# Output stores on two queues, and one store instead of two for the last tokens of both halves

## The chip, the cores and the metric

The kernel runs on one core of one Trainium2 chip. The metric is device time in microseconds (us), lower is better. Executions of one kernel mostly agree within a few tenths of a per cent. Each run is marked fast or slow by its time; of all runs told here one was slow, and only fast ones are compared.

## The reference, cut to what matters

The input `x` has 8 batches of 4224 tokens of 192 float32 values. A causal convolution of 7 taps with softmax weights per head is followed by a token-by-token mixing matrix, a relu and an output projection. The result has the shape of `x`, so 26 MB come in and 26 MB go out.

```python
x_unf = x_pad[:, idx, :].reshape(B, S, K, H, group)      # 7 shifted copies
x = einsum('hk,bskhg->bshg', w, x_unf).reshape(B, S, D)  # per-head convolution
W_tok = scale * einsum('bsd,btd->bst', x @ w_q, x @ w_k)
out = maximum(einsum('bst,btd->bsd', W_tok, x), 0.0) @ w_out
```

## The kernel before

The kernel treats each batch as two halves of 2112 tokens. Its output leaves in pieces numbered `n = 5 * b + i`: four tiles of 512 tokens of both halves (`i` 0 to 3, one store of 768 KB each) and a remainder (`i == 4`), the last 64 tokens of each half, as two stores of 48 KB. In the last batch tile 3 is the last to be computed and leaves as four quarters, in order to start storing before all of it is there. This is the code that makes the stores, all on SyncE's queue (`"sp"`):

```python
at = (b * S + 512 * i) * D
if rem:
    parts = [(at + h * HALF * D, [[D, 64], [1, D]], OUT[64 * h : 64 * h + 64, orr, 0, 0:D])
             for h in range(2)]
elif tail:
    parts = [(at + q * D, [[4 * D, 128], [HALF * D, 2], [1, D]], ...)]      # a quarter
else:
    parts = [(at, [[4 * D, 128], [HALF * D, 2], [1, 4 * D]], OUT[:, orr, :, :])]
for at, dims, src in parts:
    st = P.dma("sp", lambda e, ...: e.dma_start(bass.AP(out_t, at, dims), src), og[orr], evs + wait)
```

`dims` is the access pattern in DRAM, outermost dimension first, as `[step, count]`. `OUT` has 128 partitions and `NO = 8` slots: the copy that fills a slot waits until the store of eight pieces earlier has landed. Two more couplings matter below. Some stores also wait for loads (`GATES`, cut below): piece 10 is held back until the first loads of batch 6 have landed. And SyncE issues in order, so a store held back holds back all that follow.

```python
GATES = {0: 8, 3: 9, 5: 10, 10: 12, 15: 14}   # store n waits for a group of loads
...
P.op("sp", lambda e: e.nop(), og)             # the kernel's end: every store has landed
```

## Time and profile before

| what | before |
|---|---|
| time, median of 3 runs | 153.7 us (153.67 to 154.07) |
| profiled span | 152.5 us (of an execution of 154.32 us) |
| TensorE busy | 92% of the span |
| last copy into an output slot ends | 146.4 us |
| from there to the end | 6.1 us |

The prediction shows the slices, the chain and the windows. Two more views answer to lines shown later. First the page's DMA parts: the row of SyncE's hardware queue (packets, MB, share of 16 engines) and two groups of stores (count, KB each, median us from issue to landing).

```profile
q1 hardware_dynamic: 12576, 27.14, 48.9%
...
out_dram<-o_sb SPq DMA_DIRECT2D x31, 768.0 KB, 7.2
...
out_dram<-o_sb SPq DMA_DIRECT2D x16, 48.0 KB, 6.3
```

The packet count is worth remembering: data packets plus one 4-byte packet for each engine that reports a DMA done. Second, the rows of all output stores (duration of the issue in ns, minimum/median/maximum), and what SyncE waited for between 60 and 100 us (total, times, longest).

```profile
L860 SPq DMA_DIRECT2D out_dram<-o_sb x51: 372/514/2103, 49.0 to 149.1; - x51
```

```profile
SPq L166 <- DMA xw<-in_x_dram: 25.5, 2, 14.0
```

The longest wait of the last line, 14.0 us, is the gate of piece 10. SyncE got past it and issued that store at 84.10 us.

### The profile page before, as it was taken

Reading aid. Unit: us, or ns where it says so; the run is one execution under the profiler, and the core shown is the slowest. Engines: PE = TensorE matmul, PEld = TensorE weight load, DVE = VectorE, ACT = ScalarE, POOL = GpSimd, SP = SyncE. Lnnn points to the kernel's source line nnn. Section 1 sums busy time; section 2 is a strip of 40 time slices with the busy share of each in tenths; the row PEclk is TensorE's granted clock in tenths of the full one; section 3 lists DMA queues with packets and bytes.
Section 4 is the critical chain, followed back from the end, with each engine's and each line's share of the span. In section 5 each row is a group of like instructions: output and inputs, shape, how many; then the busy total and the mean of one; then the engine's idle time right before and its main releaser. Section 6 shows DMA issues by size and latency. Waiting matters only on the chain.

```text
span 152.5 us, 5699 instructions
## 1 busy us (share of the span) xinstructions
PE 140.1 (92%) x2457; PEld 101.3 (66%) x2457; DVE 120.3 (79%) x240; ACT 127.7 (84%) x213; POOL 59.2 (39%) x77
## 2 busy tenths in 40 slices
PE   5986789999999999999999999999999999999920
PEld 1466576876776767677776777678577777766710
DVE  6674899978987987888977859999998977795710
ACT  6456579999998899989979989899898888999930
POOL 7999999989854802554200022030200300000000
PEclk9999999999999999999999999999999999999997
DMA  3999999999999999999999999999999989499896
GB/s 107 254 198 180 190 187 170 195 187 194 191 192 196 212 340 339 289 191 279 342 338 225 192 337 335 318 192 290 408 394 407 377 327 344 172 394 375 307 355 201
DMA packets 49144, 40.88 MB, mean 268 GB/s; under 512 B 37472, under 2 KB 41184, under 8 KB 49120
## 3 DMA queue, kind: packets, MB, share of 16 engines
q0 software_dynamic: 36544, 13.40, 74.3%
q1 hardware_dynamic: 12576, 27.14, 48.9%
q8 instruction: 19, 0.31, 0.7%
q14 instruction: 5, 0.04, 0.1%
HBM read 27.96 MB, written 25.95 MB: 353 GB/s over the span
## 4 chain that ended last, share of the span: by engine, by line
PE 68%; DMA 13%; DVE 8%; POOL 3%; issue 2%; ACT 2%; SPq 1%; ACTq 0%; POOLq 0%
PE ps L207 68%; DMA out_dram<-o_sb 8%; DMA xw<-in_x_dram 5%; DVE y L1029 3%; POOL xw L338 2%; DVE yb L1025 2%; ACT o_sb L1029 1%; DVE qt L1029 1%; DVE zt L1033 1%; DVE zr L1033 1%; DVE m_sb L1035 1%; DVE o_sb L1029 1%; SPq L860 1%; ACT y L1029 1%; ACTq L155 0%
## 5 line engine op out<-in xcount | busy, mean ns | idle before, releaser
L207 PE MATMUL ps<-wo,zt 128*128 128x192 bf16 (+2 forms) x410 | 51.0, 267 | 0.2 <-DVE o_sb L1029 0.2
L1029 ACT COPY o_sb<-ps 128x768 f32<-128x768 f32 (+2 forms) x62 | 46.9, 771 | 4.3 <-PE ps L207 2.4
L1029 ACT CAST y<-ps 128x864 bf16<-128x864 f32 (+6 forms) x48 | 39.0, 835 | 5.5 <-PE ps L207 4.9
L207 PEld LDWEIGHTS ps<-y 128*128 128x128 bf16 (+1 forms) x864 | 35.6, 98 | 12.0 <-issue 2.4
L207 PEld LDWEIGHTS ps<-wo,zt 128*128 128x128 bf16 (+1 forms) x410 | 35.0, 114 | 10.4 <-ACT zt L1032 0.7
L207 PE MATMUL ps<-y 128*128 128x64 bf16 (+1 forms) x864 | 40.2, 193 | 1.0 <-DVE yb L1025 0.6
L1025 DVE STREAM_TRANSPOSE yb<-y 128x576 int32<-128x576 int32 x48 | 35.7, 759 | 0.1
L1029 POOL COPY y<-y 128x1152 bf16<-128x1152 bf16 x11 | 12.6, 1143 | 57.6 <-ACT y L1029 35.0
L207 PE MATMUL ps<-xw,band 128*128 128x432 bf16 (+5 forms) x192 | 32.3, 289 | 2.3 <-DMA xw<-in_x_dram 1.3
L1033 DVE TENSOR_SCALAR zt<-ps 128x512 bf16<-128x512 f32 x45 | 30.0, 680 | 4.6 <-PE ps L207 4.3
L338 POOL DMA_DIRECT2D xw<-in_x_dram x35 | 32.2, 932 | 2.0 <-POOL xw L498 1.1
L207 PE MATMUL ps<-qt,m_sb 128*128 128x512 bf16 (+2 forms) x120 | 30.9, 344 | 0.2 <-DVE qt L1029 0.2
L1032 ACT ACTIVATE zt<-ps 128x512 bf16<-128x512 f32 x51 | 29.8, 605 | 1.3 <-PE ps L207 1.1
L1029 DVE CAST y<-ps 128x864 bf16<-128x864 f32 (+2 forms) x20 | 20.5, 1026 | 4.9 <-PE ps L207 4.3
L207 PEld LDWEIGHTS ps<-xw,band 128*128 128x128 bf16 x192 | 13.6, 99 | 8.4 <-DMA xw<-in_x_dram 1.6
L1029 DVE CAST qt<-ps 128x288 bf16<-128x288 f32 (+1 forms) x32 | 12.2, 424 | 8.1 <-PE ps L207 7.9
L207 PE MATMUL ps<-yb,wq 32*64 32x288 bf16 x768 | 15.2, 284 | 0.5 <-DVE y L1029 0.3
L1029 ACT CAST qt<-ps 128x576 bf16<-128x576 f32 x16 | 10.3, 642 | 4.7 <-PE ps L207 4.0
L207 PEld LDWEIGHTS ps<-yb,wq 32*64 32x64 bf16 x768 | 10.6, 102 | 2.8 <-issue 0.7
L207 PEld LDWEIGHTS ps<-qt,m_sb 128*128 128x128 bf16 (+1 forms) x120 | 9.0, 96 | 4.8 <-ACT qt L1029 0.9
L1029 DVE COPY o_sb<-ps 128x192 f32<-128x192 f32 (+2 forms) x12 | 7.4, 613 | 1.3 <-PE ps L207 1.0
L207 PE MATMUL ps<-warm 128*128 128x256 bf16 (+1 forms) x22 | 6.8, 434 | 1.3 <-DVE warm L389 1.3
(62 smaller groups left out, 66.6 us busy)
## 6 DMA issues: line engine op xcount, KB each, us to landing
out_dram<-o_sb SPq DMA_DIRECT2D x31, 768.0 KB, 7.2
xw<-in_x_dram POOLq DMA_DIRECT2D x14, 432.0 KB, 15.3
xw<-in_x_dram POOLq DMA_DIRECT2D x14, 384.0 KB, 16.7
o_sb<-in_x_dram SPq DMA_DIRECT2D x2, 480.0 KB, 4.7
out_dram<-o_sb SPq DMA_DIRECT2D x16, 48.0 KB, 6.3
out_dram<-o_sb SPq DMA_DIRECT2D x4, 192.0 KB, 2.4
xw<-in_x_dram POOLq DMA_DIRECT2D x2, 240.0 KB, 6.7
xw<-in_x_dram POOLq DMA_DIRECT2D x1, 288.0 KB, 6.9
```

What stands on the lines that cost most here:

```text
L207: return self.e.matmul(*a, **k)
L338: return e.dma_start(XW[lo:hi, b % NX, half, c : c + n, :], bass.AP(x_t, at, [[D, hi - lo], [CW * D, n], [1, D]]),)
L860: lambda e, at=at, dims=dims, src=src: e.dma_start(bass.AP(out_t, at, dims), src),
L1025: return e.transpose(o, i)
L1029: return e.copy(o, i) if eng == "act" else e.tensor_copy(o, i)
L1032: return e.activation(o, i, AF.Relu)
L1033: return e.tensor_scalar(o, i, 0.0, None, op0=ALU.max)
L1035: else e.tensor_scalar(o, i, scale, None, op0=ALU.mult))
```

## The change

The intent is to shorten the end. SyncE's last seven issues lie close behind each other; three of the four quarters go to ScalarE's queue, which is free after its last copy, and the remainder leaves in one issue rather than two.

```diff
             if rem:
-                parts = [(at + h * HALF * D, [[D, 64], [1, D]], OUT[64 * h : 64 * h + 64, orr, 0, 0:D])
-                         for h in range(2)]
+                parts = [(at, [[HALF * D, 2], [D, 64], [1, D]], OUT[:, orr, 0, 0:D])]
...
             for at, dims, src in parts:
-                st = P.dma("sp", <issue>, og[orr], evs + wait)
+                if tail and q:
+                    ends.append((f, og[orr], evs + wait))
+                    st = Op("act", f, ())
+                else:
+                    st = P.dma("sp", f, og[orr], evs + wait)
...
+    for f, grp, deps in ends:
+        P.dma("act", f, grp, deps)
     P.op("sp", lambda e: e.nop(), og)
```

`ends` puts the three issues behind everything else on ScalarE. The merged store is made in every batch, eight times, and not only at the end.

> **What bounds the kernel now.** I read the page first, then the chain of work that ended last in order of time, then a table of windows from 52 us on, then the DMA view of two short windows, and last the rows of single stores in the trace.
>
> The page's slices come first: TensorE and the DMA engines side by side.
>
> ```profile
> PE   5986789999999999999999999999999999999920
> DMA  3999999999999999999999999999999989499896
> GB/s 107 254 198 180 190 187 170 195 187 194 191 192 196 212 340 339 289 191 279 342 338 225 192 337 335 318 192 290 408 394 407 377 327 344 172 394 375 307 355 201
> ```
>
> Each figure is one fortieth of 152.5 us. TensorE is full until its last two slices, so the middle is TensorE's. But the DMA row is full as well. The 16 DMA engines are the second resource with next to no room, and they alone own the last slice and a half.
>
> The chain's last pieces say who owns the end (start us, us, what):
>
> ```profile
> 67.39 12.50 DMA out_dram<-o_sb
> ...
> 140.07 5.48 PE ps L207 x44
> 145.55 0.02 issue
> 145.57 0.48 ACT o_sb L1029
> 146.05 0.38 ACTq L155
> ```
>
> Arithmetic is over at 146.4; the remaining 6.1 us are stores landing. The piece at 67.39 is the one place in mid-run where an output store that had not landed held up the copy that was to reuse its slot (ScalarE waited 0.8 us for it at 79.9).
>
> Windows: engine-busy columns, then granted clock, DMA share, GB/s.
>
> ```profile
> 52.00:64.00 12.00, 12.00 (x262) 8.59 (x255) 9.64 (x17) 11.27 (x24) 3.94 (x5) 1.00 1.19 324
> 64.00:70.00 6.00, 6.00 (x77) 4.29 (x76) 5.17 (x10) 5.38 (x10) 3.31 (x4) 1.00 1.59 193
> 107.00:125.00 18.00, 17.81 (x317) 12.73 (x316) 15.88 (x31) 16.13 (x25) 2.29 (x2) 1.00 1.02 394
> 125.00:133.00 8.00, 8.00 (x152) 6.18 (x151) 6.30 (x13) 6.86 (x12) 0.00 (x0) 1.00 0.64 236
> 133.00:141.00 8.00, 7.79 (x108) 5.37 (x105) 5.98 (x13) 7.56 (x14) 0.00 (x0) 1.00 1.02 387
> 141.00:142.00 1.00, 1.00 (x11) 0.82 (x9) 0.78 (x2) 0.92 (x2) 0.00 (x0) 1.00 0.36 111
> 148.00:149.00 1.00, 0.00 (x0) 0.00 (x0) 0.00 (x0) 0.00 (x0) 0.00 (x0) 1.00 0.79 237
> ```
>
> A share above 1 means that packets of loads and stores overlap; near 1 or above there is no idle time. Up to 125 us the engines never rest. After it the rest is 0.36 x 8 = 2.9 us in 125 to 133, 0.6 in 141 to 142 and 0.2 in 148 to 149: **3.7 us in all**.
>
> **How many engines one store uses.** The first DMA of the kernel loads 8 rows of 28 bytes. This is the DMA view of 0 to 2.2 us, in which nothing else moved:
>
> ```profile
> DMA packets 16, 0.00 MB, mean 0 GB/s; under 512 B 16, under 2 KB 16, under 8 KB 16
> q1 hardware_dynamic: 16, 0.00, 0.4%
> ```
>
> In the trace these are 8 packets of 28 bytes and 8 of 4 bytes, the semaphore writes. Every other DMA of this queue, the old 64-row stores included, made 16 semaphore writes. A DMA whose outer dimension is 8 therefore ran on 8 engines.
>
> And the DMA view of 150 to 151 us, when only the 768-byte rows of the last stores move:
>
> ```profile
> DMA packets 446, 0.33 MB, mean 327 GB/s; under 512 B 20, under 2 KB 446, under 8 KB 446
> ```
>
> 446 less 20 semaphore writes are 426 rows in 1 us on 16 engines: 26.6 each, **37.6 ns for a row of 768 bytes on one engine**.
>
> **What the Trainium skill says.** "DMA: Bandwidth & Descriptors", section "Why a DMA increments its semaphore by 16 and not by 1": a DMA is spread over the largest k up to 16 that divides the slowest dimension, not of size 1, of both access patterns, and from the hardware queues it takes the lowest-numbered k engines. The trace agrees for k (8 rows: 8 semaphore writes); it doesn't number engines, so which ones isn't shown. Same page, "Rules for kernel authors": an outermost dimension below 16 confines the whole DMA to at most that many engines. Same page, "Issuing engines are not separate DMA queues": issuing from several engines saves issue time only, all run on the same 16. The trace of before has stores from one queue only, so it can't say.
>
> **The change part by part.**
>
> Part A, the queue. The last seven issues of SyncE start at 145.10 (a 768 KB store), 145.51 and 146.07 (the two 64-row stores), 147.45, 148.09, 148.60 and 149.14 (the quarters). The second 64-row store took 1.33 us to issue. Landings of the quarters: 149.90, 150.44, 151.01, 151.57, spaced 0.56. A quarter is 256 rows, 16 an engine: 16 x 37.6 ns = 0.60 us of engine time. So the spacing is already the engines' pace, and earlier issue can only fill the hole of 148 to 149: 0.2 us. ScalarE issues its three behind its last copy (146.44), at about 0.5 us each, so from 146.5 to 148, instead of 148.1 to 149.6. The quarter copied by VectorE is ready at 145.81 and now waits for ScalarE too, at no cost. **Part A is worth about -0.2 us.**
>
> Part B, the merged store, is not only at the end: it is made for every batch, eight times. It saves eight issues of SyncE (0.47 to 1.8 us each), which matter only at the end, and there are within Part A's hole. But the memory side of the merged store is 2 halves x 64 rows x 768 bytes, outer dimension 2, while before each store had 64 outside. The SBUF side has 128 rows. The built program keeps exactly this 2 x 64. By the rule k goes from 16 to **2**: 64 rows on each of two engines.
> - before: two stores of 64 rows, 8 rows an engine: 8 x 37.6 ns = 0.30 us;
> - after: 64 x 37.6 ns = 2.41 us on two engines, nothing on the other fourteen;
> - extra on these two: 2.11 us a batch, **8 x 2.11 = 16.8 us**.
>
> Every other store needs all 16 engines and lands when its slowest does, so the two set the pace of all. They have 3.7 us of rest to absorb it: 16.8 - 3.7 = **13.1 us** later at the end. Against this a step model that I made from the trace (one engine, loads and stores taking turns packet by packet, the ready times of before, a copy waiting for its slot's store of eight before): it gives 152.4 us for the last landing of before (measured 151.57) and +12.5 us for the change, with copies waiting about 3 us in all around 92 to 120 us. I take +12.5 less 0.2: **166.0 us**.
>
> Unchanged: TensorE's, VectorE's and GpSimd's instructions and their order; ScalarE gets the three issues at its end.
>
> **The rivals.**
> 1. The merged store still spreads over 16 engines, because something below the kernel splits the rows anew. For: 128 partitions on the SBUF side. Against: the built program has 2 x 64, and the 8-row load was not split anew either. Time then: only Part A, 153.4 us.
> 2. Two engines, but a different pair each time, or the pair has rest that a mean over 16 hides. Then the 16.8 us spread and a batch costs some of its 2.11 us only when it meets a full engine: 156 to 160 us. For: nothing in the profile. Against: the page's lowest-numbered k.
> 3. Two engines, and SyncE is blocked besides. Issues already stretch when work is queued (2.1 us at 103.8, 1.9 at 118.3, against 0.37 undisturbed). With 64 rows queued on one engine the issue could hold until they drain, and later stores reach the other engines with gaps; TensorE could also stand, since the first load group of batch 7 landed at 102.9 and is used at 105.4. Up to 170 us.
> 4. Stores are slack in mid-run and only the last merged store counts: +2.1 less rest, 155.5 us. For: just one slot wait of 0.8 us in the page. Against: the rest is 3.7 us, and a queue that never empties carries delay forward whether or not anybody waits for it.
>
> **Range and chances.** I give the two-engine account (with or without rival 3) 0.8, rival 2 or 4 about 0.09, rival 1 about 0.11. Centre 166.0, range 159 to 170. Within 2% is 150.6 to 156.8, where rivals 1 and 4 lie: 0.13. Faster 0.01, slower 0.86.
>
> **What would show it right or wrong.** In the new trace: each merged store makes 2 semaphore writes by DMA instead of 16, and packets of 768 bytes go on long after most engines are done; in 107 to 152 us the mean DMA share falls well below 1 and GB/s below 390 while stores queue up; landing times of the 768 KB stores grow from 7 us; copies into the output slots wait for DMA; the end after the last copy grows from 6.1 us to over 10. If the merged stores make 16 semaphore writes, Part B is wrong and the time is 153.4. If they make 2 and the end is near 156, the carrying forward is wrong. The quarters' issues by ScalarE should take about 0.5 us each and start at 146.5 plus whatever the copies are late.

## The result, and the profile after

Ratios are the mean time of one kernel's fast runs over the mean of the other's in the same rounds, so they aren't quite the ratio of the medians quoted beside them.

| | before | after |
|---|---|---|
| time, median | 153.88 us (153.67 to 154.52, 4 runs) | 163.75 us (163.12 to 164.92, 4 runs) |
| ratio | | 1.0643 (95% interval 1.0574 to 1.0711) |
| profiled span | 152.5 us | 161.3 us |
| last copy ends | 146.44 us | 149.88 us |
| from there to the end | 6.1 us | 11.4 us |

The change costs 9.9 us. The two profiles lie only 8.8 us apart, since the one of before is of an execution of 154.32 us and this one of the fastest of four, 163.12. Of these 8.8 us, 3.4 are there when the last copy ends, and 5.4 are added behind it. The slices of the page after, each a fortieth of 161.3 us:

```profile
PE   6987889999999999999999939999999999999000
DMA  3999999999999999999999999959997796998960
GB/s 106 259 192 182 191 185 191 191 191 192 191 193 191 335 339 291 196 303 343 317 202 189 278 341 337 133 141 385 374 383 311 269 390 233 364 374 237 388 204 28
```

There is one dent in TensorE's row (the 3, at 93 to 97 us). The GB/s row has three low stretches: 133 and 141 at 101 to 109 us, several slices of 233 to 311 later, and 28 in the last slice. Before, the last slice still moved 201.

**Who carries the merged store.** The queue rows and the groups of stores of the page after:

```profile
q1 hardware_dynamic: 11520, 26.54, 45.8%
q10 hardware_dynamic: 816, 0.59, 1.1%
...
out_dram<-o_sb SPq DMA_DIRECT2D x31, 768.0 KB
...
out_dram<-o_sb SPq DMA_DIRECT2D x8, 96.0 KB
```

q10 is ScalarE's queue. Together there are 12336 packets, 240 fewer than before. The data rows are the same, so the difference is reports of done: 8 x (32 - 2) = 240 if each merged store is reported by 2 engines where its two forerunners made 32 reports (16 each). In the trace each merged store has two such packets. The one of batch 7, issued at 149.28, has them at 159.65 and 160.20, and no other packet of it is a report. The semaphore of an output slot had 96 updates by DMA before (four large stores and two small, 16 each) and has 67 after: 4 x 16, and 3 for the merged store. The Trainium skill, "DMA: Bandwidth & Descriptors", section "Why a DMA increments its semaphore by 16 and not by 1", says that the issuing sequencer writes the count of the engines not used itself, at once; two engines and one such write make the 3. This is also why nothing in the kernel's counting failed. The page now leaves the "us to landing" column of the stores empty; in e3 below, where all 16 engines report again, it is filled.

**What the two engines do at the end.** First the window of 155 to 160 us (columns as in the prediction), then the DMA view of 158.8 to 159.8 us.

```profile
155.00:160.00 5.00, 0.00 (x0) 0.00 (x0) 0.00 (x0) 0.00 (x0) 0.00 (x0) 0.50 0.21 67
```

```profile
DMA packets 61, 0.05 MB, mean 46 GB/s; under 512 B 1, under 2 KB 61, under 8 KB 61
## 3 DMA queue, kind: packets, MB, share of 16 engines
q1 hardware_dynamic: 61, 0.05, 13.6%
```

The compute engines are done, and 0.21 of 16 engines is busy. In the last full microsecond only SyncE's queue moves anything: 61 packets less 1 report are 60 rows of 768 bytes by two engines, 30 each, **33.3 ns a row on one engine**. The prediction used 37.6 ns, read from a microsecond in which all 16 engines moved such rows.

**Why compute ends later.** The waits of SyncE between 60 and 100 us, then waits of the whole span, and from the chain in order of time the stretch that holds the loss:

```profile
SPq L166 <- DMA xw<-in_x_dram: 29.8, 2, 18.2
```

```profile
ACT o_sb L1032 <- DMA out_dram<-o_sb: 2.9, 1, 2.9
PE ps L207 <- ACT o_sb L1032: 2.5, 1, 2.5
```

```profile
86.69 7.86 DMA out_dram<-o_sb
...
94.63 0.81 ACT o_sb L1032
...
143.51 5.48 PE ps L207 x44
...
149.02 0.48 ACT o_sb L1032
```

Read from the top: the loads that gate piece 10 landed later, so that SyncE got past its gate at 86.69 instead of 84.10. Two merged stores (issued at 53.5 and 67.9) had been made by then. The gated store landed 7.9 us later; before, it took 7.1. The copy of piece 18, which reuses its slot, waited 2.9 us for that landing, and TensorE waited 2.5 us for the copy. That is the dent. From there on the whole of compute is late. The table of windows shows a second thing in the same place:

```profile
92.00:96.00 4.00, 1.55 (x20) 0.93 (x19) 2.75 (x4) 1.37 (x2) 0.00 (x0) 0.97 1.15 341
96.00:100.00 4.00, 4.00 (x75) 2.53 (x74) 1.11 (x3) 2.65 (x5) 1.15 (x1) 0.61 1.14 339
107.00:125.00 18.00, 17.81 (x323) 12.88 (x322) 16.22 (x34) 16.08 (x24) 2.29 (x2) 1.00 0.95 353
```

TensorE's granted clock averages 0.61 over 4 us right after it stood (the trace's clock record has 0.50 from 95.74 us for 3.4 us). Two experiments below with the same dent (e2 and e4) have 1.00 there and lose 2.0 us of compute instead of 3.4, so about 1.5 us of this profile's loss seem to go with the clock; no run tests this. The last row shows the stores' side: from 107 to 125 us DMA was at 1.02 and 394 GB/s before and is at 0.95 and 353 now, although stores were outstanding: the one issued at 120.29 landed 12.4 us later, and the same store before, issued at 118.30, landed 6.4 us later.

**Issues.** The rows of all output stores, as shown of before:

```profile
L858 SPq DMA_DIRECT2D out_dram<-o_sb x40: 372/524/5448, 48.8 to 150.3; - x40
L858 ACTq DMA_DIRECT2D out_dram<-o_sb x3: 424/1156/1282, 149.4 to 151.0; - x3
```

One issue held SyncE for 5.4 us (at 120.29), others for 4.2 (110.99) and 3.7 (150.28). An undisturbed one takes 0.37. It looks as if SyncE could not hand the other fourteen engines the next store while two have a long queue. What holds an issue isn't shown, though, and e7 below loses 3.3 us without any long issue.

### The profile page after: what moved, and what is told of

It is laid out like the page before. It is cut to its first block, busy times and chain, and to the rows that moved or that the text cites. A ratio compares the mean times of both kernels' runs of the same rounds, so it can differ in the third digit from the quotient of the medians.

```text
span 161.3 us, 5691 instructions
## 1 busy us (share of the span) xinstructions
PE 141.5 (88%) x2457; PEld 101.8 (63%) x2457; DVE 120.2 (75%) x240; ACT 127.9 (79%) x213; POOL 59.1 (37%) x77
## 4 chain that ended last, share of the span: by engine, by line
PE 67%; DMA 10%; DVE 8%; ACT 4%; POOL 2%; issue 1%; ACTq 0%; POOLq 0%
PE ps L207 67%; DMA out_dram<-o_sb 5%; DMA xw<-in_x_dram 5%; DVE y L1032 2%; POOL xw L338 2%; ACT o_sb L1032 2%; DVE yb L1028 1%; DVE qt L1032 1%; DVE zt L1036 1%; DVE zr L1036 1%; DVE m_sb L1038 1%; ACT zt L1035 1%; DVE o_sb L1032 1%; ACT y L1032 0%; ACT qt L1032 0%
## 5 line engine op out<-in xcount | busy, mean ns | idle before, releaser
L207 PE MATMUL ps<-yb,wq 32*64 32x288 bf16 x768 | 15.9, 293 | 0.3 <-DVE y L1032 0.3
L207 PEld LDWEIGHTS ps<-yb,wq 32*64 32x64 bf16 x768 | 10.9, 106 | 2.9 <-issue 0.7
```

Of the source, the lines that this page charges most:

```text
L207: return self.e.matmul(*a, **k)
```

## The experiments

Two claims are to be separated. The theory: a merged store runs on two engines because its pattern in DRAM has 2 outside, and this alone costs the time. Rivals: the second queue costs it; one large store instead of two small ones costs it whatever its width; only the last one counts; or the cost is spread evenly over all eight. All outputs were correct. The kernels e1 to e4, e5 to e8 and e9 to e10 each shared a chip and the runs of before, whose median was 154.25, 154.20 and 154.26 us.

### e1: the queue alone

The remainder is in two stores again; only `ends` is left of the change.

```diff
-parts = [(at, [[HALF * D, 2], [D, 64], [1, D]], OUT[:, orr, 0, 0:D])]
+parts = [(at + h * HALF * D, [[D, 64], [1, D]], OUT[64 * h : 64 * h + 64, orr, 0, 0:D])
+         for h in range(2)]
```

> The queue part alone: three quarters issued by ScalarE, the 64-row stores as before. Theory (width: the 64 rows on each of two engines cost the time): about 0.2 us faster than before, 153.5 us, because the quarters already land at the engines' pace. Rival (the second queue costs or gains the time, by two queues taking turns on one engine): clearly slower than before, up to the 163.8 of the whole change.

Measured: 154.19 us, ratio 0.9995 (0.994 to 1.005, 5 rounds). The queue rows of its page:

```profile
q1 hardware_dynamic: 11760, 26.55, 47.8%
q10 hardware_dynamic: 816, 0.59, 1.2%
```

They add up to 12576, exactly the count before, so the width of every store is as it was. The second queue neither gains nor costs anything that shows. The Trainium skill, "DMA: Bandwidth & Descriptors", section "Issuing engines are not separate DMA queues", says that a second issuing engine saves issue time only. This run agrees, and here even the issue time saved was worth nothing measurable.

### e2: the merge alone

All stores are on SyncE's queue; the remainder is merged as in the change.

```diff
-if tail and q:
-    ends.append((f, og[orr], evs + wait))
-    ...
-else:
-    st = P.dma("sp", f, og[orr], evs + wait)
+st = P.dma("sp", <issue>, og[orr], evs + wait)
```

> The merged store alone, everything issued by SyncE. Theory (width): the whole loss, 163.8 us within 0.5. Rival (second queue): 153.7 us. If the two parts interact at the end, between them.

Measured: 166.97 us, ratio 1.0827 (1.0754 to 1.09). The merge carries the whole loss, and more: this kernel is some 3 us slower than the full change, which the expectation missed. Two views of its trace, the rows of the stores and the DMA view of its last 3.6 us of transfers, 160.3 to 163.9:

```profile
L859 SPq DMA_DIRECT2D out_dram<-o_sb x43: 372/654/6227, 48.3 to 157.4; - x43
```

```profile
DMA packets 117, 0.08 MB, mean 23 GB/s; under 512 B 7, under 2 KB 117, under 8 KB 117
```

23 GB/s is half of what the two engines moved at the end of the change: one engine was left alone. It had fallen behind its partner earlier. Of the store issued at 139.45 fourteen engines reported by 145.6, one at 147.15 and one at 150.20; for the stores before it the two were 0.8 us apart. Around 146.2 single packets of 3072 bytes took up to 2.1 us there. The change's own trace has packets of up to 1.7 us at 146.3. What causes these I could not find. The trace of before has such a packet too, of 1.28 us at 126.2, so they don't come from the merge alone.

### e3: the merge, on sixteen engines

The remainder leaves in one store as in the change, but its rows are laid out so that token outside and half inside is the order in DRAM too. The relu's copy interleaves the halves over the partitions to match.

```diff
-parts = [(at, [[HALF * D, 2], [D, 64], [1, D]], OUT[:, orr, 0, 0:D])]
+parts = [(at, [[D, 64], [HALF * D, 2], [1, D]], OUT[:, orr, 0, 0:D])]
```

> The whole change, but the last tokens' rows stand as 2s+h on the partitions, so that the one merged store has 64 rows outside and 2 halves inside. Theory (width): 16 semaphore writes per merged store, 8 rows an engine, and the loss is gone: 153.4 us. Rival (one store of both halves is slow as such, being one long issue or one long transfer whatever its engines): stays at 163.8.

Measured: 153.62 us (153.31 to 153.93), ratio 0.9953 (0.9902 to 1.0003, 5 rounds). The whole loss is gone. The lines of its page:

```profile
q1 hardware_dynamic: 11632, 26.55, 47.7%
q10 hardware_dynamic: 816, 0.59, 1.3%
...
out_dram<-o_sb SPq DMA_DIRECT2D x8, 96.0 KB, 7.8
```

12448 packets are 128 fewer than before, 8 x (32 - 16): one store with 16 reports in place of two. The bytes, the rows, the number of stores and the queues are those of the change; only which dimension is outside differs. This is the version to keep of the three ideas, though its interval touches 1, so it isn't shown to beat the kernel before.

### e4: two stores again, each on two engines

If two engines are the cause and merging isn't, two unmerged stores with 2 outside must lose as much. Each half's 64 tokens are split into even and odd ones, and the relu's copy is rearranged to match.

```diff
-parts = [(at, [[HALF * D, 2], [D, 64], [1, D]], OUT[:, orr, 0, 0:D])]
+parts = [(at + h * HALF * D, [[D, 2], [2 * D, 32], [1, D]], OUT[64 * h : 64 * h + 64, orr, 0, 0:D])
+         for h in range(2)]
```

> The merge undone (two stores of 64 rows, as before), but each with 2 outside: rows even and odd, 32 rows on each of two engines per store, 64 rows an engine per batch as in the change. Theory (width): 2 semaphore writes per store and about the time of the change, 163.8 us within 1. Rival (the merge as such costs the time): 153.5 us.

Measured: 166.07 us, ratio 1.0755 (1.0668 to 1.0843), without one slow run of 169.36. Its packets, 11536 + 816, are 224 fewer than before: 16 x (16 - 2). So the loss follows the two engines and not the merge. The rearranged copy isn't it either: e5 below has one of the same kind and loses 1.1 us. Like e2 this kernel is worse than the change, by 1.8 us if the ratios are compared (11.7 us over before against 9.9), and outside the 1 us that was expected.

### e5: two stores, each on four engines

As e4, with 4 outside: `[[D, 4], [4 * D, 16], [1, D]]`. Each of four engines gets 32 rows a batch instead of 64 on two.

> Like the two stores with 2 outside, but with 4 outside: 16 rows on each of four engines per store, 32 rows an engine per batch instead of 64. Theory (width, with the 3.7 us of rest spent once): 24 rows more than before, at 32 to 37 ns, eight times, is 6.2 to 7.1 us, less 3.7: 2.5 to 3.4 us over before, about 157 us. Rival (a DMA on fewer than 16 engines costs a fixed amount, however few): near the 166 us of two engines. Rival (loss in proportion to the extra rows, nothing absorbed): 24/56 of 12 us, 5 us over before.

Measured: 155.41 us, ratio 1.0073 (1.0038 to 1.0108), 1.1 us more than before. The packets are 192 fewer, 16 x (16 - 4). The direction held; the size was expected larger. So more of the added engine time found rest than I had assumed: 32 rows of about 35 ns (an estimate between the 33.3 and the 37.6) less the 0.30 us of before are 0.8 us a batch, 6.6 in eight, of which 5.5 didn't show.

### e6, e7 and e8: merged in some batches only

The merged form is used for `b < 4`, for `b >= 4`, and for the last batch alone.

```diff
-parts = [<merged>]
+parts = [<merged>] if b < 4 else [<the two stores>]      # e7: b >= 4; e8: b == B - 1
```

> The change, but merged on two engines only in batches 0 to 3; the last four batches store 2 x 64 rows as before. Theory (delay carried forward on two engines, rest spent once): 4 x 1.8 us less 3.7 us of later rest is 3.4 us over before, about 157.5 us. Rival (each merged store costs the same): half of the change's loss, 5 us over. Rival (only the last stores count): 0 over.

> The change, but merged only in batches 4 to 7. Theory (carried forward, rest spent once): again about 3.4 us over before, no copy waiting at 94 us; the two halves together then lose about 7 where the whole loses 10, as the rest is spent in each. Rival (each costs the same): 5 us over. Rival (only the last stores count): the whole 10 us over.

> The change, but merged only in the last batch. Theory: the last store's own extra of 1.8 us, less the 0.2 us hole: 1.6 us over before. Rival (only the last merged store counts): the change's whole 10 us over.

| | merged in | median us | ratio | over before |
|---|---|---|---|---|
| e6 | first four | 156.50 | 1.0145 (1.0109 to 1.0182) | 2.2 us |
| e7 | last four | 157.40 | 1.0212 (1.0177 to 1.0248) | 3.3 us |
| e8 | last one | 156.82 | 1.0175 (1.0138 to 1.0211) | 2.7 us |

(The last column is the ratio's excess times 154.2. By the 2% rule of the verdicts e6, like e5, counts as the same and e7 and e8 as unclear, but all these intervals exclude 1.) The wait that e6 shows, the gate of SyncE in e6 and in e7, 60 to 100 us, and the row of SyncE's stores in e7:

```profile
ACT o_sb L1034 <- DMA out_dram<-o_sb: 2.8, 1, 2.8
```

```profile
SPq L166 <- DMA xw<-in_x_dram: 30.2, 2, 18.6
```

```profile
SPq L166 <- DMA xw<-in_x_dram: 26.0, 2, 14.4
```

```profile
L860 SPq DMA_DIRECT2D out_dram<-o_sb x44: 372/510/1554, 48.0 to 145.7; - x44
```

With the first four merged, the gate opens late (the store behind it goes at 87.00 us), the copy waits and the last copy ends at 148.5: the loss is the shift of compute. With the last four merged the gate opens as before (83.60), no copy waits for a store, and the last copy ends at 145.8: the loss is all behind it. So the change loses in two separate places. In e7 no issue of SyncE took over 1.55 us, less than the longest before (2.10), so two engines cost time even where SyncE isn't held. e6 loses less than the 3.4 us expected and e7 as much as expected; their sum, 5.5 us, is less than the 9.9 of the whole. The rest (idle time of the DMA engines that takes up part of the delay) would explain that: each uses it for itself, while the whole can use it only once. This is argued, not shown.

e8 lost 1 us more than expected. Its merged store landed at 151.88 and 152.25, its last quarter at 153.54 on the two engines but by 151.2 on the others. A merged store with nothing behind it to hide under costs its full extra time, and here 0.9 us more than the 1.8 of 64 rows; that 0.9 I can't place (in the two profiles the last landings lie only 2.0 us apart). And e8 alone loses 2.7 of e7's 3.3 us: merging batches 4 to 6 besides adds only some 0.6 us, with overlapping intervals. In that half nearly all that shows is the last store.

### e9 and e10: can the end be shortened in another way?

Both use e3's layout on SyncE's queue alone. e9 stores the last tile whole, in rows of 3072 bytes; e10 stores it as two, in rows of 1536. The output slot is filled in the order that this needs.

```diff
-parts = [(at + q * D, [[4 * D, 128], [HALF * D, 2], [1, D]], ...)]
+parts = [(at + (q - 3) * D, [[4 * D, 128], [HALF * D, 2], [1, 4 * D]],      # e9; e10: 2 * D, q - 1
+          OUT[:, orr, :, D * (q - 3) : D * q + D])]
```

> A version meant to beat both: the merged store spread over 16 engines, no second queue, and the last four quarters as one store with rows of 3072 bytes instead of four with rows of 768. The engines are busy with earlier stores until 148.4 us, two us after the last copy, so waiting for all four quarters costs nothing, and 16 rows of 125 ns are 2.0 us where 64 of 37.6 ns are 2.4. Expected 0.4 to 0.7 us faster than before. Rival (earlier issue of the quarters matters): slower than before by up to 1 us.

> As the version with one last store, but with two of rows of 1536 bytes. Engine time between the two: about 0.2 us gained on before by the rows and 0.2 by the hole; expected 0.3 to 0.6 us faster than before, within 0.3 of the one-store version.

Measured: 154.12 us, ratio 1.0001 (0.9974 to 1.0028), and 154.15, ratio 1.0002 (0.9977 to 1.0027), 5 rounds each. Neither gains the few tenths expected. The quarters of the kernel before are as good as longer rows that have to start later.

## Why the prediction was right or wrong

Direction and size were predicted: 166.0 us, range 159 to 170, measured 163.75. By its own steps:

- **Part A about nothing:** right. Predicted -0.2 us, e1 measured -0.1 within plus or minus 0.9.
- **k goes from 16 to 2 (against rival 1):** right, by the count of reports, and e3 shows that the order of two dimensions decides it. Rival 1 fell.
- **Always the same two (against rival 2):** every batch's delay landed on the same pair as far as the landings tell, since in the large stores two reports come late as a rule (of the one issued at 120.29 fourteen by 129.51, two at 132.09 and 132.67). The trace doesn't number engines. Rival 2's 156 to 160 us did not come.
- **The delay is carried forward (against rival 4):** right for the whole change, which ends 11.4 us behind its last copy where e8, with only the last store merged, ends 8.6 behind it: the seven others are felt at the end too. But the prediction let the queue carry the delay "whether or not anybody waits for it", and the halves don't show that. e6 ends 6.3 us behind its last copy (6.1 before), so nothing of its four merged stores is left in the queue; its 2.2 us came through the copy that waited. And in e7 batches 4 to 6 add only some 0.6 us to the last store's 2.7.
- **The size of one row:** this is the mis-sized term. The prediction took 37.6 ns, which gave 16.8 us in all; with the two engines alone a row took 33.3 ns. Then 64 x 33.3 ns less the 0.30 us of before are 1.83 us a batch, 14.6 in all, and less 3.7 of rest 10.9 instead of 13.1. The rest was also under-sized. In the change 14.6 - 9.9 = 4.7 us didn't show, in e6 7.3 - 2.2 = 5.1, in e7 4.0, in e5 5.5. With some 4 to 5.5 the sum is 9 to 10.6, and the change measured 9.9. This is no independent test: the 4.7 us are taken from the change itself, e6 lost by another path, and that a row takes 33.3 ns in mid-run too is assumed. That the mean over 16 engines missed idle time of the pair is likely but not shown. The step "near 1 or above there is no idle time" doesn't hold as a reading of the windows: the share counts overlapping packets, 1.59 at 193 GB/s against 1.02 at 394, so a share near 1 can contain idle time.
- **The step model's copies waiting about 3 us around 92 to 120 us:** right, one wait of 2.9 us ending at 94.6. But the route is one that the step model, which has no gates, couldn't give, so the agreement is partly luck: the merged stores delay loads, the loads open a store's gate late, and that store's slot is the one waited for.
- **SyncE blocked besides (rival 3):** seen, up to 5.4 us for one issue. e7 shows that two engines cost time without it; how much it adds in the change isn't separated.
- **More than 10 us behind the last copy:** right, 11.4.
- **A slip without effect:** the eight issues saved took 0.60 to 1.80 us before, not 0.47 to 1.8.

What stays open: e2 and e4 have the same two engines and the same rows, and lose 12.8 and 11.7 us, not 9.9. In both the last microseconds belong to one engine alone, at 17 to 26 GB/s, so the pair had come apart, which the sum of rows doesn't give. SyncE was also held longer in both: its store issues after 100 us, less 0.37 us each, sum to 30 us in e2 and in e4, 20 in the change and 15 before. Which of these causes which isn't shown. With three kernels of one kind spread over 3 us, the agreement of the corrected sum with the change is better than the account deserves. That the dip of the clock to 0.61 is in the change's profile and in neither of theirs makes the gap larger, not smaller.

## What to carry to other kernels

Before merging two transfers, look at which dimension ends up outside. If it is small, the DMA runs on as few engines (here 2, 4 and 8 outside ran on 2, 4 and 8), and every later transfer that needs all engines waits for those few, also the loads, whose delay can reach compute through gates and slots far away. Merge with the long dimension outside, and count the 4-byte reports of done in the queue's packet count, which gives away the width of transfers on the page alone.

## What the Trainium skill lacked or had wrong

- "DMA: Bandwidth & Descriptors", section "Rules for kernel authors", advises one transfer over 128 partitions instead of two to disjoint halves, since both run on all 16 engines anyway. Followed without the page's own rule on the outermost dimension, this lost 9.9 us (1.0643), because the merge put 2 outside; with 64 outside (e3) the ratio is 0.9953. The row should say so.
- No page gives the time of a row of 768 bytes in a store to DRAM on one engine: 37.6 ns with all 16 engines at it, 33.3 ns with two.
- No page gives how long the issue of one store can get while others are queued: 5.4 us after the change, 6.2 in e2, 0.37 undisturbed.
- "TensorE: Matmul & The Clock Gate" doesn't account for a half clock after a single stand as short as here: the clock record has 0.50 for 3.4 us after a stand of 2.45 us in one profile (the change's), and no drop after 2.62 us in e2 and e4 and 2.41 in e6.
